# Moving a memset and retuning the constants of a build-time scheduler in a fused attention and MLP kernel

## Chip, cores, metric

One core of a Trainium2 chip. The metric is the device time of one execution in microseconds, as the median over the runs; a profiled execution also gives a span (first to last instruction), about 1.8 us shorter. A ratio between two kernels is the mean time of one kernel's fast runs over that of the other's fast runs of the same rounds, so it is not quite the ratio of the medians quoted beside it.

## The reference

Two branches share one layer-normed input and are added to it: softmax attention with 32 heads of 16, and an MLP that mixes over the sequence.

```python
S, D, H, Dh, F = 2048, 512, 32, 16, 1376
xn  = layernorm(x)
# A: q, k, v = split(xn @ wqkv);  o = softmax(q k^T / sqrt(Dh)) v;  A = o @ wo
# B: h = layernorm(xn);  u = gelu(h^T @ w1 + b1);  B = (u @ w2 + b2)^T
out = x + A + B            # bf16, (1, 2048, 512)
```

The 32 heads' scores are 32 x 2048 x 2048 exponentials. As the profile below shows, they fill one engine, and the matrix products fill another.

## The kernel before

The exponentials are cut into 1024 score tiles of 128x1024. ScalarE takes most of them with its exponential, one per instruction. VectorE takes the others by an integer trick: one instruction from PSUM, and three shifted copies, two usually on GpSimd and one on VectorE. A VectorE tile therefore needs four groups of PV matmuls (the exponentials times V) on TensorE, a ScalarE tile one.

The whole program is laid out at build time by a list scheduler. It walks a model of the five engines with fixed costs, and writes one instruction stream per engine. The engines run their streams in order, so a constant of the model changes what is in the streams. These are the parts that the change touches (cuts marked):

```python
PE_SWITCH = 0.11          # model: TensorE changes between row-tiled scores and column-tiled other work
DMA_I, DMA_L = 0.6, 3.5   # model: issue and landing of a DMA
D_LATE = 1.0              # how late VectorE asks for its next score tile
ACT_MIN = 0.5             # filler matmuls are put in where TensorE's modelled activity is below this
# ...
def est(specs):                        # when could this instruction start
    for s_ in specs:
        r = max(r, sc.ready(s_["eng"], s_["reads"], s_["writes"]))
# ...
def fill(t_next, same):                # matmuls without use, to hold the TensorE clock
    if cur_ext is not None or last_n is None or sc.pe_activity(t_next) > ACT_MIN:
        return
# ...   TensorE's choice: next score tile, or a PV or extra group first?
wants = [sc.free["act"] + EXP_I * i for i in range(4)]
if fly < D_FLY and len(free_p) >= 4 + P_KEEP:
    wants.append(sc.free["dve"] + backlog(sc.free["dve"]) + D_LATE)
need = sorted(wants)[ahead] - 0.46 - DEAD_SLACK
# ...
if pick is not None and pick[0] + pick[4] + PE_SWITCH <= go + PE_FIT:
    pe_c = pick[:4]                    # the group fits before the score tile is due
```

"Extra" work is everything else on TensorE: Q, K and V projections, the MLP's first product ("ut"), and the 16 output tiles ("fin": MLP's second product and the attention output product). Each extra task has a due date, counted in score tiles (0 to 1023).

The head, as code:

```python
ln_sums(1)
warm_up(N_WARM, 5)                                   # 11 matmuls without use
sc.add("pool", lambda e: e.memset(v17_main[:, :, 16:17], 1.0), ...)   # the ones column of V
ln_stats(0)                                          # VectorE statistics, GpSimd 1/sqrt ("rstd")
# ... statistics of tiles 1 to 3, their rstds
for t in range(NPRE):
    ln_norm(t)                                       # VectorE, four normalisations
late_memsets()                                       # GpSimd, zeros in VM
for t in range(NPRE):
    transpose_pe(t, TB[t])
# ... copies to SBUF, Q and K products, first scores, first exponential
```

The softmax here doesn't subtract the row's maximum and nothing guards it: scores larger than these inputs give would overflow.

Of the kernel before, what the change touches and what calls it, by code (L numbers as in the profile page):

```python
# [21 lines left out]
NT = S // 128  # L22
# [3 lines left out]
NQB = 4  # L26
NG = 8
NKT = 16
NBLK = NQB * NG
# [16 lines left out]
NXB = 8  # L46
NW = 2
NPRE = 4
N_WARM = 11


SEM = 0.05
PE_SWITCH = 0.11
PE_LAT = 0.40
EXP_I, EXP_L = 0.903, 1.03
P1_I, P1_L = 1.13, 1.22
TS_I, TS_L = 0.335, 0.42
TT_I, TT_L = 0.60, 0.685
EV_I, EV_L = 0.61, 0.69
DMA_I = 0.6  # L60
DMA_L = 3.5
SH_I, SH_L = 0.62, 0.70
HN_I, HN_L = 0.20, 0.29
OT_I, OT_L = 0.60, 0.685
# [1 line left out]
D_FLY = 3  # L66
D_BACK = 0.5
D_STEAL = 0.3
D_LATE = 1.0
P_KEEP = 4  # L70
DEAD_SLACK = 0.1
PORT_SLACK = 0.5
PE_FIT = 0.05
TABLE = 1.3
LIB_I = 7.2
Q_LEAD = 52
KV_LEAD = 16
HARD_HOLD = 10
LATE_BY = 0
EX_FROM = 34  # L80
EX_RATE = 0.15
EX_EARLY = 10
GELU_GAP = 16
ACT_WIN = 3.42
ACT_MIN = 0.5
# [23 lines left out]
class Sched:  # L109
# [36 lines left out]
            deps = {d for d in deps if d.eng != "pe" or d.is_dma}  # L146
        return deps

    def ready(self, eng, reads, writes, dma=False):

        t = 0.0
        for d in self._deps(eng, reads, writes, dma):
            t = max(t, d.t1 + (SEM if d.eng != eng or d.is_dma else 0.03))
        return t

    def port_time(self, eng, t):
# [150 lines left out]
def bass_parallel_sum__softmax_full_mha__mixer_token_mlp__prompt_kernel(  # L307
# [18 lines left out]
    with ExitStack() as es:  # L326
# [164 lines left out]
        def ln_stats(t):  # L491
            sc.add("dve", lambda e: e.bn_stats(stats[:, t, :], x_sb[:, t, :]),
                   reads=[("x", t)], writes=[("stats", t)], cost=(0.6, 0.69))
            sc.add("dve", lambda e: e.bn_aggr(mv[:, t, 0:2], stats[:, t, :]),
                   reads=[("stats", t)], writes=[("mv", t)], cost=(0.12, 0.18))
            ln_rstd(t, 1)
# [51 lines left out]
        def transpose_pe(t, bk):  # L548
            for ct in range(NCT):
                sc.add("pe", lambda e, ct=ct: e.transpose(  # L550
                    ps_bf[:, bk * 1024 + ct * 128: bk * 1024 + (ct + 1) * 128],
                    xn_sb[:, t, ct * 128:(ct + 1) * 128], ident[:]),
                    reads=[("xn", t), ("ident",)], writes=[("bank", bk)], cost=("F", (0, 1, 2, 3), 0.06))
# [69 lines left out]
               writes=[("rcomp", 0)], cost=(1.4, 1.5))  # L623
        ln_sums(1)
        warm_up(N_WARM, 5)
        sc.add("pool", lambda e: e.memset(v17_main[:, :, 16:17], 1.0), writes=[("Vone",)], cost=(0.5, 0.6))  # L626
        ln_stats(0)
        sc.add("dve", lambda e: e.bn_stats(stats[:, 2, :], x_sb[:, 2, :]), reads=[("x", 2)], writes=[("stats", 2)], cost=(0.6, 0.69))
        sc.add("dve", lambda e: e.bn_aggr(mv[:, 2, 0:2], stats[:, 2, :]), reads=[("stats", 2)], writes=[("mv", 2)], cost=(0.12, 0.18))
        ln_moments(1)  # L630
        ln_rstd(1, 2)
        ln_stats(3)
        for t in range(NPRE):
            ln_norm(t)
        late_memsets()
# [1 line left out]
        TB = (0, 1, 2, 3)  # L637
        for t in range(NPRE):
            transpose_pe(t, TB[t])
        for t in range(NPRE):  # L640
            transpose_copy(t, TB[t], "dve" if t == 2 else "act")
        ln_stats(NPRE)
# [370 lines left out]
        oT_done = set()  # L1013
# [65 lines left out]
        def pv_ready(b):  # L1079

            best = None
            for it in pv_q.get(b, ()):
                if not pv_has(it):
                    continue
                t = sc.last_writer[("pT", it[2])].t1 + SEM
                if best is None or t < best[0]:
                    best = (t, it)
            return best
# [39 lines left out]
        while hard or soft or fins:  # L1128
            tail_ = 0.0
            slack_ = 1e9  # L1130
            for due, cost, *_r in hard:
                tail_ += cost
                slack_ = min(slack_, due - cur - tail_ / EX_RATE)
            nxt = soft[0] if soft else (fins[0] if fins else None)
            if nxt is not None and (not hard or slack_ > nxt[0] / EX_RATE):
                cost, nm, gen, need = (soft or fins).pop(0)
                rel = 0
            else:
                due, cost, nm, gen, need, rel = hard.pop(0)
            cur = max(cur, rel) + cost / EX_RATE  # L1140
            ext_tasks.append((max(rel, cur - cost / EX_RATE - EX_EARLY), cur, nm, gen, need))
            if nm == "ut" and not soft:
                cur += GELU_GAP
        ext_tasks.sort(key=lambda z: z[1])

        def h_mark(t):
# [42 lines left out]
                g["cur"] = (kind, what)  # L1189
                return  # L1190

        def est(specs):
            s0 = specs[0]
            r = 0.0
            for s_ in specs:
                r = max(r, sc.ready(s_["eng"], s_["reads"], s_["writes"]))
            t = max(sc.free[s0["eng"]], r)
            if s0.get("port"):
                t = sc.port_time(s0["eng"], t)
            return t  # L1200
# [21 lines left out]

        def fill(t_next, same):

            if cur_ext is not None or last_n is None or sc.pe_activity(t_next) > ACT_MIN:
                return
            if sc.ready("pe", [], [("bank", EX_BANK)]) > sc.free["pe"]:
                return
            b, kt, qb, G, T, e_ = blk_of(last_n)
            r = 2  # L1230
            if sc.pe_mode == "S" and len(sc.pe_tiles) <= 2 and r not in sc.pe_tiles and not same:
                sc.add("pe", lambda e: e.matmul(
                    bank(EX_BANK), lhsT=KT[32 * r:32 * r + 32, T, 128 * kt:128 * (kt + 1)],
                    rhs=QT[32 * r:32 * r + 32, b % 4, :], start=True, stop=True, tile_position=(32 * r, 0)),
                    reads=[("KTt", T, kt), ("QT", b % 4, r)], writes=[("bank", EX_BANK)], name="fill",
                    cost=("S", (r,), 0.214))
            for _ in range(int((t_next - sc.pe_end - 2 * PE_SWITCH - 0.1) / 0.22)):
                sc.add("pe", lambda e: e.matmul(bank(EX_BANK), lhsT=ident[:], rhs=wo_c[:, 0, :], start=True, stop=True),
                       reads=[("ident",)] + [("wo_c", x, r) for x in range(2) for r in range(4)],
                       writes=[("bank", EX_BANK)], name="fill", cost=("F", (0, 1, 2, 3), 0.22))  # L1240
# [5 lines left out]
        while True:  # L1246
            cands = []

            for g in frees:
                if g["cur"] and g["cur"][0] == "sp":  # L1250
                    w = g["cur"][1][0]
                    cands.append((max(sc.free["sp"], sc.ready("sp", w["reads"], w["writes"], dma=True)), 0, "dma", g))
# [68 lines left out]
                    jobs.append((max(t_c, a[0], sc.ready("pe", [], [("bank", PV_BANK)])), 0 if low else 2, "pv", a[1], 0.107))  # L1321
            if cur_ext and cur_ext["cur"] and cur_ext["cur"][0] == "pe":
                late = next_n - min([cur_ext["due"]] + [z[1] - HARD_HOLD for z in ext_tasks if z[2] in ("qt", "kt", "vt")])
                jobs.append((max(t_c, est(cur_ext["cur"][1])), 1 if late > -LATE_BY else 3, "ext", cur_ext, 0.214))
            pick = None
            if jobs:
                m = min(j[0] for j in jobs)
# [1 line left out]
            if sp_ is not None:  # L1329
                ahead = len(ready_q)  # L1330
# [4 lines that stand above are left out]
                two = sorted(slot_time(z) for z in free_slots)  # L1335
                if sc.pe_mode == "S" and e_s <= sc.pe_end + 0.02:
                    go = e_s
                else:
                    t2 = two[1] if len(two) > 1 else 1e9
                    if len(two) == 1:  # L1340
                        t2 = 1e9
                    go = max(e_s, min(need, t2))
                if pick is not None and pick[0] + pick[4] + (PE_SWITCH if sc.pe_mode == "C" else PE_SWITCH) <= go + PE_FIT:
                    pe_c = pick[:4]
                elif pick is not None or True:
                    pe_c = (max(e_s, go if go < 1e8 else e_s), 0, "score", (next_n, sp_, s_))
            elif pick is not None:
                pe_c = pick[:4]
# [93 lines left out]
            if cur_ext is None:  # L1442
                for i, (rel, due, nm, gen, need) in enumerate(ext_tasks):
                    if rel > next_n:
                        continue
                    if need and need[0] == "ut" and (need[1] != len(u_begun) or len(h_done) < NT):
                        continue
                    if need and need[0] == "fin":
                        if need[1] >= 12 and not (("q", NBLK - 2) in have and (NQB - 1, 1) in oT_done):
                            continue  # L1450
                        if need[1] != fin_next or not all(("g", ft) in have for ft in range(NFT)):
                            continue
                        fin_next += 1
                    if nm == "ut":
                        u_begun.append(need[1])
                    ext_tasks.pop(i)
                    cur_ext = dict(gen=gen, cur=None, due=due, name=nm)
                    step_gen(cur_ext)
                    break
# [62 lines left out]
```

## Time and profile before

| | |
|---|---|
| time | 706.06 us (704.78 to 706.14, 3 runs; 706.02 with the fourth) |
| first exponential on ScalarE | 12.95 us |
| last exponential ends | 691.8 us |
| last PV group issued | 693.0 us |
| end of the span | 704.3 us |
| score tiles on ScalarE / VectorE | 725 / 299 |

From the page of the kernel before: its span, the busy times, the chain of work that ended last, and the groups of the exponentials (busy us and mean ns of one; then idle time before them and what ended most of it).

```profile
span 704.3 us, 29187 instructions
PE 688.5 (98%) x12808; PEld 325.6 (46%) x12808; DVE 607.0 (86%) x879; ACT 680.4 (97%) x744; POOL 391.3 (56%) x666
...
PE 73%; ACT 19%; DVE 3%; issue 2%; SPq 2%; POOL 1%; DVEq 0%; DMA 0%; POOLq 0%
...
L737 ACT ACTIVATE pT<-ps 128x1024 bf16<-128x1024 f32 x522 | 515.4, 1151 | 3.8 <-PE ps L713 3.2
...
L748 DVE TENSOR_SCALAR pT<-ps 128x1024 int16<-128x1024 f32 x207 | 252.9, 1222 | 32.7 <-PE ps L713 23.6
...
L737 ACT ACTIVATE x_sb<-ps 128x1024 bf16<-128x1024 f32 x203 | 221.8, 1159 | 1.1 <-PE ps L713 0.9
...
L748 DVE TENSOR_SCALAR x_sb<-ps 128x1024 int16<-128x1024 f32 x92 | 112.4, 1222 | 15.3 <-PE ps L713 10.8
```

ScalarE has under 5 us of idle before its 725 exponentials: it is full. VectorE has 34.4 us of idle before its 299 tiles that a score matmul ended (23.6+10.8). The chain is mostly TensorE. A busy TensorE is not yet a full one, so look at a short stretch near the end of the body. This is the chain of the kernel before (start us, us, what):

```profile
684.41 0.21 PE ps L810 x4
...
686.57 0.32 PE ps L713 x2
686.89 0.33 PE ps L810 x4
687.22 0.41 PE ps L713 x4
687.64 0.77 PE ps L780 x24
688.41 0.32 PE ps L713 x2
```

From 686.57 on each piece starts where the last one ends, with a period of 1.84 us: two score runs (L713), one extra group (L810), six PV groups (L780). In 1.84 us ScalarE does two tiles and VectorE one. So TensorE and ScalarE are both full here. An extra group that follows a score run costs 0.33 us, while eleven in a row cost 2.55 us, some 0.22 each (below), and the group at 684.41, which follows a PV group in the same tiling mode, costs 0.21: the other 0.10 to 0.12 us go with the change of tiling mode. The Trainium skill ("TensorEngine Tiling (Array Packing)", "Key Properties") says that a change of tiling mode drains TensorE; the trace agrees so far as such a change costs 0.10 to 0.12 us.

The head of the kernel before, from its timeline (start us, us, engine, line, operation). L626 is the V-ones memset, L522 the fourth normalisation, L431 the VM memsets, L601 Q products, L737 the first exponentials:

```profile
2.72 2.29 POOL L626 MEMSET V<- 128x512 bf16 x1
...
7.96 0.87 DVE L522 TENSOR_SCALAR hx<-x_sb,mv 128x512 bf16<-128x512 bf16 x1
...
7.88 0.80 POOL L431 MEMSET VM<- 128x256 bf16 x3
...
10.14 1.48 PE L601 MATMUL ps<-xnT,wq_sb 128*128 128x128 bf16 x12
...
12.95 3.77 ACT L737 ACTIVATE pT<-ps 128x1024 bf16<-128x1024 f32 x4 [0.81 <-PE ps L713]
```

Normalisation 4 takes 0.87 us where the median of the sixteen is 0.38; it lies over three GpSimd memsets and ends 0.15 us after they do. The Q products run 0.107 us apart, and the granted clock in the windows from 9 to 12 us is 0.50: half clock.

The tail of the kernel before, from its timeline. L810 is extra work (the last output tile), L1043 an operation on VectorE that feeds the last matmuls L1059:

```profile
693.12 2.55 PE L810 MATMUL ps<-gT_sb,wblk 128*32 128x512 bf16 x44
...
695.67 0.42 DVE L1043 TENSOR_TENSOR oT<-ps,oC 128x256 bf16<-128x256 f32 x1
695.93 0.39 PE L810 MATMUL ps<-xr,ident 128*32 128x512 bf16 x4
...
698.41 1.03 PE L1059 MATMUL ps<-wo_t,oT 128*128 128x512 bf16 x4
```

VectorE's operands are there at 696.1 us, but TensorE is in the last output tile until 696.3 and, after four other products and six matmuls that only hold the clock (left out), reaches the last products at 698.41.

### The profile page before, as it was taken

The page shows a single profiled execution, that of the slowest core. Times are in us where ns is not written, and L with a number is a line of the kernel's source. Part 1 is how long each engine was busy: PE and PEld are TensorE (multiplying, and loading weights), DVE is VectorE, ACT ScalarE, POOL GpSimd, SP SyncE. Part 2 cuts the span into 40 slices and gives each one's busy share as a digit, 9 for nine tenths or more (in the row PEclk, how much of TensorE's full clock was granted, in tenths as well). Part 3 has the DMA queues.
Part 4 walks back from the last instruction along what each step waited for, and adds up shares of the span by engine and source line. Part 5 has one row for each costly group of instructions (what it writes and reads, how often), then busy time and mean ns, then how long its engine had stood idle before and what let it go on. Part 6 is the DMA issues. An engine that isn't in the chain of part 4 may idle for free.

```text
span 704.3 us, 29187 instructions
## 1 busy us (share of the span) xinstructions
PE 688.5 (98%) x12808; PEld 325.6 (46%) x12808; DVE 607.0 (86%) x879; ACT 680.4 (97%) x744; POOL 391.3 (56%) x666
## 2 busy tenths in 40 slices
PE   7999999999999999999999999999999999999998
PEld 4533544444444454444444454444544444445444
DVE  6968889888897889989889998979899888988886
ACT  5999999999999999999999999999999999999993
POOL 5535446565564636556565674546556564665551
PEclk9999999999999999999999999999999999999999
DMA  7103200221002200211221023112221121222211
GB/s 210 32 19 69 51 23 14 52 49 27 15 14 53 48 23 18 43 36 36 49 42 44 19 47 72 48 39 53 54 55 35 43 66 41 53 55 54 48 43 47
DMA packets 85727, 32.31 MB, mean 46 GB/s; under 512 B 67424, under 2 KB 85600, under 8 KB 85600
## 3 DMA queue, kind: packets, MB, share of 16 engines
q1 hardware_dynamic: 85168, 30.05, 18.4%
q8 instruction: 100, 1.64, 1.0%
q10 hardware_dynamic: 432, 0.39, 0.2%
q14 instruction: 27, 0.22, 0.1%
HBM read 21.76 MB, written 2.35 MB: 34 GB/s over the span
## 4 chain that ended last, share of the span: by engine, by line
PE 73%; ACT 19%; DVE 3%; issue 2%; SPq 2%; POOL 1%; DVEq 0%; DMA 0%; POOLq 0%
PE ps L780 27%; PE ps L713 27%; PE ps L810 15%; ACT pT L737 13%; ACT x_sb L737 4%; SPq L404 2%; PE ps L859 1%; DVE pT L748 1%; ACT gT_sb L914 1%; PE ps L619 0%; DVE oT L1006 0%; PE ps L563 0%; PE ps L550 0%; DVE x_sb L748 0%; POOL V L626 0%
## 5 line engine op out<-in xcount | busy, mean ns | idle before, releaser
L737 ACT ACTIVATE pT<-ps 128x1024 bf16<-128x1024 f32 x522 | 515.4, 1151 | 3.8 <-PE ps L713 3.2
L713 PE MATMUL ps<-QT,KT 32*128 32x512 bf16 x2048 | 291.0, 384 | 5.0 <-ACT pT L737 3.0
L748 DVE TENSOR_SCALAR pT<-ps 128x1024 int16<-128x1024 f32 x207 | 252.9, 1222 | 32.7 <-PE ps L713 23.6
L754 POOL INT64_ADD pT<-pT x307 | 185.6, 613 | 147.1 <-DVE pT L757 80.9
L780 PE MATMUL ps<-pT,V 128*32 128x256 bf16 x4632 | 237.9, 275 | 0.9 <-ACT pT L737 0.6
L737 ACT ACTIVATE x_sb<-ps 128x1024 bf16<-128x1024 f32 x203 | 221.8, 1159 | 1.1 <-PE ps L713 0.9
L713 PEld LDWEIGHTS ps<-QT,KT 32*128 32x128 bf16 x2048 | 86.5, 91 | 179.2 <-ACT pT L737 80.6
L780 PEld LDWEIGHTS ps<-pT,V 128*32 128x32 bf16 x4632 | 109.9, 96 | 68.0 <-issue 52.1
L748 DVE TENSOR_SCALAR x_sb<-ps 128x1024 int16<-128x1024 f32 x92 | 112.4, 1222 | 15.3 <-PE ps L713 10.8
L780 PE MATMUL ps<-x_sb,V 128*32 128x256 bf16 x1856 | 115.1, 275 | 0.3 <-ACT x_sb L737 0.3
L754 POOL INT64_ADD pT<-x_sb x128 | 77.4, 613 | 56.8 <-DVE pT L757 32.6
L754 POOL INT64_ADD x_sb<-pT x114 | 69.4, 613 | 44.8 <-DVE pT L757 31.0
L757 DVE TENSOR_SCALAR pT<-pT 128x1024 int16<-128x1024 int16 x149 | 63.4, 428 | 4.5
L780 PE MATMUL ps<-pT,VM 128*32 128x256 bf16 x884 | 61.2, 274 | 0.0
L810 PE MATMUL ps<-hx,wblk 128*32 128x512 bf16 x688 | 60.5, 384 | 0.0
L810 PE MATMUL ps<-gT_sb,wblk 128*32 128x512 bf16 (+1 forms) x704 | 58.4, 383 | 0.7 <-DVE hx L948 0.7
L780 PEld LDWEIGHTS ps<-x_sb,V 128*32 128x32 bf16 x1856 | 47.3, 96 | 24.2 <-issue 18.1
L754 POOL INT64_ADD x_sb<-x_sb x58 | 35.3, 613 | 28.4 <-DVE pT L757 8.1
L757 DVE TENSOR_SCALAR pT<-x_sb 128x1024 int16<-128x1024 int16 x66 | 27.9, 424 | 2.1
L810 PEld LDWEIGHTS ps<-hx,wblk 128*32 128x32 bf16 x688 | 16.2, 94 | 24.1 <-issue 21.1
L780 PEld LDWEIGHTS ps<-pT,VM 128*32 128x32 bf16 x884 | 23.6, 97 | 6.6 <-issue 6.1
L810 PEld LDWEIGHTS ps<-gT_sb,wblk 128*32 128x32 bf16 (+1 forms) x704 | 16.3, 95 | 20.8 <-issue 16.1
(105 smaller groups left out, 397.4 us busy)
## 6 DMA issues: line engine op xcount, KB each, us to landing
wblk<-in_B_w_dram SPq DMA_DIRECT2D x10, 512.0 KB, 4.6
wblk<-in_B_w_dram SPq DMA_DIRECT2D x16, 320.0 KB, 3.6
oC<-OT SPq DMA_DIRECT2D x248, 16.0 KB, 1.8
denb<-rden_scratch SPq DMA_DIRECT2D x124, 32.0 KB, 2.0
xr<-in_A_x_dram SPq DMA_DIRECT2D x16, 128.0 KB, 2.3
dcomp<-OT SPq DMA_DIRECT2D x124, 2.0 KB, 1.8
QT<-Qall SPq DMA_DIRECT2D x120, 16.0 KB, 1.8
out_dram<-osb SPq DMA_DIRECT2D x14, 128.0 KB, 1.9
```

The lines of the kernel that those rows point to most:

```text
L404: return eng.dma_start(dst, src)
L713: specs.append(dict(eng="pe", fn=lambda e, r=r, bk=bk: e.matmul(bank(bk), lhsT=KT[32 * r:32 * r + 32, T, 128 * kt:128 * (kt + 1)], rhs=QT[ ...
L737: return [dict(eng="act", fn=lambda e: e.activation(buf(pbuf[n]), ps[:, s_ * 1024:(s_ + 1) * 1024], ACTF.Exp, scale=LN2_128), reads=[("ban ...
L748: return dict(eng="dve", fn=lambda e: e.tensor_scalar(buf_i(w), ps[:, s_ * 1024:(s_ + 1) * 1024], IBIAS, 0.0, ALU.add, ALU.max), reads=[(" ...
L754: return dict(eng=eng, fn=lambda e: e.int64_add(buf_i(o).bitcast(I64), buf_i(w).bitcast(I64), SHIFTS[k] * 0x0001000100010001), reads=[("pT ...
L757: return dict(eng=eng, fn=lambda e: e.tensor_scalar(buf_i(o), buf_i(w), float(SHIFTS[k]), 1.0, ALU.add, ALU.mult), reads=[("pT", w)], writ ...
L780: specs.append(dict(eng="pe", fn=lambda e, c=c, h=h, i=i, off=off: e.matmul(bank(PV_BANK)[32 * c:32 * c + 32, 256 * par:256 * par + 256], ...
L810: specs.append(dict(eng="pe", fn=lambda e, c=c, w=w: e.matmul(bank(EX_BANK)[32 * c:32 * c + w, :], lhsT=lhs_of(32 * c, 32 * c + w), rhs=rh ...
L859: specs.append(dict(eng="pe", fn=lambda e, ct=ct, c=c, i=i, t=t: e.matmul(bank(EX_BANK)[32 * c:32 * c + 32, 128 * i:128 * (i + 1)], lhsT=x ...
L914: yield "act", [dict(eng="act", fn=lambda e, ap=ap: e.activation(ap, ap, ACTF.Gelu_apprx_tanh), reads=[("gT", f) for f in fts], writes=[(" ...
```

## The change

The intent: free GpSimd's first rstd from the memset; keep the TensorE clock up in the head; give VectorE its score tiles sooner; have the last output tiles done before the end; let work fed by other engines or by DMA have a margin in the model. The diff, cut to its core:

```diff
-N_WARM = 11
+N_WARM = 13
+N_MID = (1, 1, 1, 2)
-PE_SWITCH = 0.11
+PE_SWITCH = 0.1
-DMA_I = 0.6
-DMA_L = 3.5
+DMA_I = 0.65
+DMA_L = 3.0
+DMA_SLACK = 0.8
+EXT_SLACK = 0.2
+PV_SLACK = 0.1
-D_LATE = 1.0
+D_LATE = 0.5
+Q_GUARD = 8
+FIN_END = 985
+FIN_STEP = 18
@@ head
         warm_up(N_WARM, 5)
-        sc.add("pool", lambda e: e.memset(v17_main[:, :, 16:17], 1.0), writes=[("Vone",)], cost=(0.5, 0.6))
         ln_stats(0)
# ... 
         ln_rstd(1, 2)
         ln_stats(3)
+        sc.add("pool", lambda e: e.memset(v17_main[:, :, 16:17], 1.0), writes=[("Vone",)], cost=(2.28, 2.33))
         for t in range(NPRE):
             ln_norm(t)
# ...
             transpose_pe(t, TB[t])
+            warm_up(N_MID[t], 5)
@@ scheduler
+        for i, z in enumerate(ext_tasks):
+            if z[2] == "fin":
+                due = min(z[1], FIN_END - (NT - 1 - z[4][1]) * FIN_STEP)
+                ext_tasks[i] = (min(z[0], due - 30),) + (due,) + z[2:]
-        def est(specs):
+        def est(specs, slack=0.0):
-                r = max(r, sc.ready(s_["eng"], s_["reads"], s_["writes"]))
+                r = max(r, sc.ready(s_["eng"], s_["reads"], s_["writes"], slack=slack, dma_slack=DMA_SLACK))
-                t = sc.last_writer[("pT", it[2])].t1 + SEM
+                t = sc.last_writer[("pT", it[2])].t1 + SEM + PV_SLACK
# ...   extra tasks
+                    if nm in ("ut", "fin") and any(z[2] == "qt" and z[0] < next_n + Q_GUARD for z in ext_tasks):
+                        continue
-                        if need[1] >= 12 and not (("q", NBLK - 2) in have and (NQB - 1, 1) in oT_done):
+                        if need[1] >= 12 and ("q", NBLK - 2) not in have:
# (smaller hunks left out: query DMAs first on the queue, no fillers once the last output tile has begun)
```

More of the change, by code (lines that the diff above doesn't have):

```diff
@@ L59 @@
 EV_I, EV_L = 0.61, 0.69
-DMA_I = 0.6
-DMA_L = 3.5
+DMA_I = 0.65
[3 more added lines that the diff above has]
+PV_SLACK = 0.1
+GEN_SLACK = 0.0
 SH_I, SH_L = 0.62, 0.70
@@ L68 @@
 D_STEAL = 0.3
-D_LATE = 1.0
+D_LATE = 0.5
 P_KEEP = 4
 DEAD_SLACK = 0.1
+PAIR_WAIT = 0.0
 PORT_SLACK = 0.5
@@ L147, in _deps, with ready @@
         return deps
-    def ready(self, eng, reads, writes, dma=False):
+    def ready(self, eng, reads, writes, dma=False, slack=0.0, dma_slack=0.0):
         t = 0.0
         for d in self._deps(eng, reads, writes, dma):
-            t = max(t, d.t1 + (SEM if d.eng != eng or d.is_dma else 0.03))
+            t = max(t, d.t1 + (SEM + (dma_slack if d.is_dma else slack) if d.eng != eng or d.is_dma else 0.03))
         return t
@@ L1223, in fill @@
         def fill(t_next, same):
-            if cur_ext is not None or last_n is None or sc.pe_activity(t_next) > ACT_MIN:
+            if cur_ext is not None or last_n is None or fin_next == NT or sc.pe_activity(t_next) > ACT_MIN:
                 return
@@ L1247, in bass_parallel_sum__softmax_full_mha__mixer_token_mlp__prompt_kernel @@
             cands = []
-            for g in frees:
+            for g in sorted(frees, key=lambda g: not (g["cur"] and g["cur"][0] == "sp" and g["cur"][1][0]["name"] == "q_row")):
                 if g["cur"] and g["cur"][0] == "sp":
@@ L1323, in bass_parallel_sum__softmax_full_mha__mixer_token_mlp__prompt_kernel @@
                 late = next_n - min([cur_ext["due"]] + [z[1] - HARD_HOLD for z in ext_tasks if z[2] in ("qt", "kt", "vt")])
-                jobs.append((max(t_c, est(cur_ext["cur"][1])), 1 if late > -LATE_BY else 3, "ext", cur_ext, 0.214))
+                jobs.append((max(t_c, est(cur_ext["cur"][1], EXT_SLACK)), 1 if late > -LATE_BY else 3, "ext", cur_ext, 0.214))
             pick = None
@@ L1341, in bass_parallel_sum__softmax_full_mha__mixer_token_mlp__prompt_kernel @@
                         t2 = 1e9
-                    go = max(e_s, min(need, t2))
+                    go = max(e_s, t2 if t2 <= need + PAIR_WAIT else need)
                 if pick is not None and pick[0] + pick[4] + (PE_SWITCH if sc.pe_mode == "C" else PE_SWITCH) <= go + PE_FIT:
```

## The prediction

> **What bounds it now.** Median 706.06 us; profiled span 704.3 us, in three parts.
>
> - Head, to the first exponential on ScalarE at 12.95 us (timeline).
> - Body, to the last exponential at 691.8 us. ScalarE is full: the waits view gives it about 4 us of idle there, and 60 us stretches hold 66 or 67 exponentials, one each 0.917 us. TensorE is full too: the chain of waits is 73% TensorE, and in the end stretch it is contiguous TensorE work with a period of 1.84 us (score runs 0.32+0.41, PV 0.77, one other 0.33), in which ScalarE does two tiles and VectorE one. VectorE is 86% busy and does 299 of 1024 score tiles, 1.22 us each; it waits 34.4 us (82 times) for scores.
> - Tail, from the last PV at 693.3 us to the end, 11 us.
>
> **Head.** The V-ones memset (GpSimd, 2.72 to 5.01 us) delays the first rstd to 5.07 (input ready at 4.13), but the first normalisation sits behind VectorE's own statistics until 6.55, so the move frees only about 0.15 us. The memset (2.29 us) will start as the fourth rstd ends, at about 7.75, just before normalisation 4. The Trainium skill ("SBUF — State Buffer", "SBUF: two separate sides") says that GpSimd and a two-port VectorE operation exclude each other for the whole instruction. This trace agrees: normalisation 4 took 0.87 instead of 0.38 us and ended 0.14 us after three GpSimd memsets did. So normalisation 4 should end near 10.2, not 8.83. Against that, the clock is at half in 8.9 to 12 us (windows), where 32 Q/K matmuls cost 0.107 us each; two more warm-ups and five between the transposes may keep it full, worth about 1.6 us. Net: first exponential at 13.0, 11.5 to 15.
>
> **Body.** Margins (0.8 us on DMA-fed, 0.2 on extra, 0.1 on PV work) change only the build-time order. The stalls they address are small (waits): TensorE's loads wait 6.7 us for GpSimd and 0.5 for a query DMA, VectorE 3.2 for denominators. Asking for VectorE's tile 0.5 us sooner attacks the 34.4 us. If half returned, VectorE could take ten more tiles (about 1.5 us each with its shift), but each costs TensorE three more PV groups (0.32 us), and TensorE is full. I give 5 to 8 more tiles, 2 to 3 us together with the margins.
>
> **Tail.** Output tile 15 is computed after the last PV (693.1 to 696.3, about 3.2 us of TensorE), so final products wait until 698.4, though VectorE's operands are there at 696.1. With it due earlier, the tail should be about 2.2 us shorter, 9 us, but the work moves into a full body and is partly paid there. Net 1.5 to 2 us.
>
> **Predicted: 701.5 us, range 696.5 to 706.5; faster by over 2%: 0.03, within 2%: 0.95, slower: 0.02.**
>
> **What would show it.** Right: normalisation 4 ends within 0.2 us of the memset's end; tail from last PV near 9 us; no output tile after the last PV; VectorE's score waits well below 34 us; 304 to 307 VectorE tiles; ScalarE still full. Wrong: first exponential near 11 us (memset doesn't block, clock stays full); a much higher tile count, which would mean TensorE had room.
>
> **What would make it wrong.** A half clock through the head (first exponential at 15 us); the new order pairing score tiles less well, costing TensorE a mode change each; early output tiles starving PV of buffers; or an order lucky by more than these sums.

## The result

| | before | after |
|---|---|---|
| time, us | 706.02 (4 runs) | 699.63 (699.18 to 701.46, 4 runs) |
| ratio, 95% interval | | 0.9918 (0.9898 to 0.9939) |
| span of the profiled run | 704.3 | 697.7 |
| first exponential | 12.95 | 14.00 |
| last exponential ends | 691.8 | 683.7 |
| last PV group issued | 693.0 | 689.5 |
| from there to the end | 11.3 | 8.2 |
| tiles on ScalarE / VectorE | 725 / 299 | 717 / 307 |

It is 6.4 us faster, 0.8%. The head got slower by 1.05 us. The last exponential ends 8.1 us sooner, but the last PV only 3.5 us sooner, and the tail behind it is 3.1 us shorter. (3.5 and 3.1 make the 6.6 us of the span.) The same views as before, first the page of the kernel after:

```profile
span 697.7 us, 29410 instructions
PE 682.8 (98%) x12914; PEld 312.1 (45%) x12914; DVE 623.2 (89%) x902; ACT 673.4 (97%) x736; POOL 397.2 (57%) x675
...
PE 58%; ACT 36%; DVE 3%; issue 1%; DMA 1%; POOL 0%; SPq 0%; DVEq 0%
...
L747 ACT ACTIVATE pT<-ps 128x1024 bf16<-128x1024 f32 x528 | 516.5, 1130 | 1.9 <-PE ps L723 0.9
L758 DVE TENSOR_SCALAR pT<-ps 128x1024 int16<-128x1024 f32 x220 | 268.7, 1222 | 23.6 <-PE ps L723 18.4
...
L747 ACT ACTIVATE x_sb<-ps 128x1024 bf16<-128x1024 f32 x189 | 203.4, 1136 | 0.5 <-PE ps L723 0.5
...
L758 DVE TENSOR_SCALAR x_sb<-ps 128x1024 int16<-128x1024 f32 x87 | 106.3, 1222 | 12.3 <-PE ps L723 9.5
```

Eight tiles went over to VectorE, whose waits for scores fell from 34.4 to 27.9 us (18.4+9.5) though there are more tiles. ScalarE is still full.

The head, from the timeline of the kernel after (L641 the V-ones memset, L531 normalisation 4, L440 and L442 the VM memsets, L610 Q products):

```profile
7.68 2.27 POOL L641 MEMSET V<- 128x512 bf16 x1
...
7.77 3.10 DVE L531 TENSOR_SCALAR hx<-x_sb,mv 128x512 bf16<-128x512 bf16 x1
...
9.55 1.11 POOL L440 MEMSET VM<- 128x256 bf16 x3
10.61 0.11 POOL L442 MEMSET VM<- 128x16 bf16 x1
...
12.04 0.83 PE L610 MATMUL ps<-xnT,wq_sb 128*128 128x128 bf16 x12
...
14.00 3.77 ACT L747 ACTIVATE pT<-ps 128x1024 bf16<-128x1024 f32 x4 [0.48 <-PE ps L723]
```

Normalisation 4 now lies over the moved memset and over the VM memsets behind it, and takes 3.10 us. In this run the clock was full: twelve Q products took 0.83 us instead of 1.48.

The tail, from the timeline of the kernel after:

```profile
685.82 2.55 PE L820 MATMUL ps<-gT_sb,wblk 128*32 128x512 bf16 x44
...
688.85 0.39 PE L820 MATMUL ps<-xr,ident 128*32 128x512 bf16 x4
...
689.50 0.28 PE L790 MATMUL ps<-pT,VM 128*32 128x256 bf16 x4
...
691.88 1.03 PE L1069 MATMUL ps<-wo_t,oT 128*128 128x512 bf16 x4
```

The last output tile still comes after the last exponential (683.7), but now ahead of the last PV groups. The final products start 2.4 us after the last PV group, not 5.4. There TensorE now waits for VectorE's operands (ready at 691.77); before, they waited for TensorE.

### The profile page after: what moved, and what is told of

Read it like the earlier page. It is cut to its first block, busy times and chain, and to the rows that moved or that the text cites. A ratio compares the mean times of both kernels' runs of the same rounds, so it can differ in the third digit from the quotient of the medians.

```text
span 697.7 us, 29410 instructions
## 1 busy us (share of the span) xinstructions
PE 682.8 (98%) x12914; PEld 312.1 (45%) x12914; DVE 623.2 (89%) x902; ACT 673.4 (97%) x736; POOL 397.2 (57%) x675
## 4 chain that ended last, share of the span: by engine, by line
PE 58%; ACT 36%; DVE 3%; issue 1%; DMA 1%; POOL 0%; SPq 0%; DVEq 0%
ACT pT L747 25%; PE ps L790 23%; PE ps L723 20%; PE ps L820 12%; ACT x_sb L747 10%; DVE pT L758 1%; ACT gT_sb L924 1%; PE ps L869 1%; DMA denb<-rden_scratch 1%; PE ps L628 1%; DVE hx L531 0%; DVE OT L980 0%; DMA x_sb<-in_A_x_dram 0%; DVE wkv_raw L1016 0%; PE ps L559 0%
## 5 line engine op out<-in xcount | busy, mean ns | idle before, releaser
L758 DVE TENSOR_SCALAR pT<-ps 128x1024 int16<-128x1024 f32 x220 | 268.7, 1222 | 23.6 <-PE ps L723 18.4
L723 PE MATMUL ps<-QT,KT 32*128 32x512 bf16 x2048 | 283.5, 384 | 6.2 <-ACT pT L747 3.7
L790 PE MATMUL ps<-pT,V 128*32 128x256 bf16 x4692 | 251.0, 275 | 1.5 <-DVE OT L980 1.2
L764 POOL INT64_ADD pT<-pT x296 | 179.7, 615 | 124.1 <-DVE pT L767 64.9
L747 ACT ACTIVATE x_sb<-ps 128x1024 bf16<-128x1024 f32 x189 | 203.4, 1136 | 0.5 <-PE ps L723 0.5
L723 PEld LDWEIGHTS ps<-QT,KT 32*128 32x128 bf16 x2048 | 76.9, 91 | 184.9 <-ACT pT L747 76.4
L764 POOL INT64_ADD x_sb<-pT x148 | 90.4, 614 | 66.3 <-DVE pT L767 41.0
L758 DVE TENSOR_SCALAR x_sb<-ps 128x1024 int16<-128x1024 f32 x87 | 106.3, 1222 | 12.3 <-PE ps L723 9.5
L767 DVE TENSOR_SCALAR pT<-pT 128x1024 int16<-128x1024 int16 x167 | 71.1, 428 | 4.7
L764 POOL INT64_ADD x_sb<-x_sb x42 | 25.6, 613 | 20.6 <-DVE pT L767 6.8
L790 PEld LDWEIGHTS ps<-pT,VM 128*32 128x32 bf16 x904 | 24.1, 96 | 11.5 <-issue 9.5
```

What stands on the lines that cost most here:

```text
L723: specs.append(dict(eng="pe", fn=lambda e, r=r, bk=bk: e.matmul(bank(bk), lhsT=KT[32 * r:32 * r + 32, T, 128 * kt:128 * (kt + 1)], rhs=QT[ ...
L747: return [dict(eng="act", fn=lambda e: e.activation(buf(pbuf[n]), ps[:, s_ * 1024:(s_ + 1) * 1024], ACTF.Exp, scale=LN2_128), reads=[("ban ...
L758: return dict(eng="dve", fn=lambda e: e.tensor_scalar(buf_i(w), ps[:, s_ * 1024:(s_ + 1) * 1024], IBIAS, 0.0, ALU.add, ALU.max), reads=[(" ...
L764: return dict(eng=eng, fn=lambda e: e.int64_add(buf_i(o).bitcast(I64), buf_i(w).bitcast(I64), SHIFTS[k] * 0x0001000100010001), reads=[("pT ...
L767: return dict(eng=eng, fn=lambda e: e.tensor_scalar(buf_i(o), buf_i(w), float(SHIFTS[k]), 1.0, ALU.add, ALU.mult), reads=[("pT", w)], writ ...
L790: specs.append(dict(eng="pe", fn=lambda e, c=c, h=h, i=i, off=off: e.matmul(bank(PV_BANK)[32 * c:32 * c + 32, 256 * par:256 * par + 256], ...
```

## Experiments

Twelve kernels ran, all correct, five rounds each. "E1" and so on are the names used below. The counts of tiles and of leftover matmuls in the expectations are counts in the built instruction streams.

### E1: the memset behind the normalisations

```diff
         ln_stats(3)
-        sc.add("pool", lambda e: e.memset(v17_main[:, :, 16:17], 1.0), writes=[("Vone",)], cost=(2.28, 2.33))
         for t in range(NPRE):
             ln_norm(t)
+        sc.add("pool", lambda e: e.memset(v17_main[:, :, 16:17], 1.0), reads=[("xn", NPRE - 1)], writes=[("Vone",)], cost=(2.28, 2.33))
         late_memsets()
```

> The kernel after, with the V-ones memset put behind normalisation 4 (it waits for it). Theory A (GpSimd's memset shuts VectorE's normalisation 4 out): normalisation 4 takes about 0.4 us again and ends near 8.2 us instead of 10.87; the first exponential starts at 11.3 us instead of 14.0; the body is in the same order and just comes earlier, so the time is about 2.7 us below the kernel after, near 697.0 us (ratio to before 0.987). Rival B (the late start comes from the extra warm-ups in TensorE's queue or from late data): first exponential still at 13.5 to 14 us, time as the kernel after, ratio 0.992.

Measured: 697.48 us, ratio 0.9874 (0.9856 to 0.9892), span 695.7. From the timeline of E1, normalisation 4 and the first exponentials:

```profile
7.74 0.41 DVE L531 TENSOR_SCALAR hx<-x_sb,mv 128x512 bf16<-128x512 bf16 x1
...
11.29 3.77 ACT L747 ACTIVATE pT<-ps 128x1024 bf16<-128x1024 f32 x4 [0.48 <-PE ps L723]
```

Normalisation 4 is back to 0.41 us and the first exponential starts at 11.29. Theory A holds, and the rival falls: the warm-ups and the loads are the same and do not delay the start. (The edit takes two things out of normalisation 4's way, for the VM memsets come behind the moved one.) Of the 2.7 us at the start 2.0 are left in the span. The rest is lost little by little: the lead over the kernel after is 2.7 us at 42 us, 2.3 at ScalarE's table load at 409 us, and 2.1 at the last exponential; what eats it is open.

### E2: the extra warm-ups undone

```diff
-N_WARM = 13
-N_MID = (1, 1, 1, 2)
+N_WARM = 11
+N_MID = (0, 0, 0, 0)
```

> The kernel after with 11 warm-ups and none between the transposes; the memset stays where the change put it. Theory A: normalisation 4 still ends near 10.9 us, and the granted clock falls to half while TensorE waits, so the Q and K products take 0.107 us each as in the kernel before, and the first exponential starts near 15.5 us: 1.5 us slower than the kernel after (ratio to before 0.994). Rival B (the warm-ups are what delays the start): first exponential near 13 us and faster than the kernel after.

Measured: 701.43 us, ratio 0.9927 (0.991 to 0.9943), span 699.2, first exponential at 14.73 us. The twelve Q products took 1.49 us, half clock. So it is not the warm-ups that delay the start: without them it should have come near 13 us. What they gain is not shown. This profile starts 0.7 us later than the kernel after's, where 1.5 were expected, but the same head with its warm-ups is at half clock too in the profiles of E7 to E9, and starts there at 15.3 to 15.4 us, later than here.

### E3: the whole head of before

```diff
-N_WARM = 13
-N_MID = (1, 1, 1, 2)
+N_WARM = 11
+N_MID = (0, 0, 0, 0)
         warm_up(N_WARM, 5)
+        sc.add("pool", lambda e: e.memset(v17_main[:, :, 16:17], 1.0), writes=[("Vone",)], cost=(0.5, 0.6))
# ... and the moved memset taken out again
```

> The kernel after with the whole head of before (memset ahead of the statistics, 11 warm-ups, none between). Theory A: the change's head costs time by itself, first exponential back at 12.95 us, time 1.0 us below the kernel after (about 698.6 us, ratio 0.9905); all of the gain, 7.5 us of the span, comes from the scheduled body. Rival (the head is part of the gain): ratio 0.993 or higher.

Measured: 699.32 us (697.75 to 699.72), ratio 0.9887 (0.9867 to 0.9907), span 697.6, first exponential at 13.49 us, Q products again at half clock. E2 and E3 differ only in the memset's place: the moved memset costs 2.1 us between their medians. The head is no part of the gain. Against the kernel after as a whole the difference (0.9887 and 0.9918) is not resolved by the intervals; compared by clock, E3's two runs with a mean clock of 1.000 took 697.75 us, and the kernel after's three took 699.2 to 699.7.

### E4: VectorE's score tile asked for as late as before

```diff
-D_LATE = 0.5
+D_LATE = 1.0
```

> The kernel after with VectorE's score tile asked for as late as before (1.0 for 0.5). The built order then has 298 VectorE tiles, not 307, and 726 on ScalarE. Theory C (the gain of the body is tiles moved from ScalarE to VectorE, 0.917 us each, and the last exponential ends that much earlier): last exponential about 8 us later than in the kernel after, near 692 us, no output tile left for after the last scores, time 2 to 6 us above the kernel after, ratio 0.995 to 1.0. Rival D (TensorE alone is the bound, so the number of VectorE tiles doesn't matter): same time as the kernel after, ratio 0.992 within 0.0015.

Measured: 704.36 us, ratio 0.9964 (0.9946 to 0.9981), span 700.6. VectorE has 298 tiles and waits 41.0 us for scores (27.9 in the kernel after). The last exponential ends about 691.7 us, as expected. No output tile is left behind the last PV, and from there to the end it is 8.2 us as in the kernel after. Theory C holds: on top of the rest of the change the sooner tile is worth 3.2 us, give or take 1.9 (difference of the two ratios; 2.9 us of the span). It is not worth the full 8 us by which the exponentials end sooner, because TensorE then has PV groups and output tiles left (from the last exponential's start to the last PV it is 1.9 us here, 7.0 in the kernel after).

### E5: the switch constant alone, on the kernel before

```diff
-PE_SWITCH = 0.11
+PE_SWITCH = 0.1
```

> The kernel before with one constant of its build-time scheduler changed: the assumed cost of a TensorE mode switch, 0.11 to 0.10 us. The built order then has 303 VectorE tiles (before 299) and leaves the same 44 matmuls of an output tile for after the last scores. Theory E (this constant decides whether an extra or PV group still fits ahead of the next score, so TensorE's gaps are filled better, and part of the body's gain is this): last exponential 3 to 4 us earlier than before, ratio to before 0.994 to 0.9955. Rival (a rounding of no effect; the gain is the sooner score tile and the margins): ratio 1.000 within 0.0015.

Measured: 707.17 us (704.02 to 709.51), ratio 1.0019 (0.9999 to 1.004). The expectation missed. VectorE had its 303 tiles, but the last exponential came only 1.3 us sooner. Its runs show mean clocks of 0.983 to 0.990, where the kernel before's beside it show 0.993 to 1.000. The next lines are windows of E5 (us; length; busy us of PE, PEld, DVE, ACT, POOL; then the granted clock, DMA share and GB/s):

```profile
46.00:50.00 4.00, 3.10 (x43) 1.00 (x31) 3.88 (x8) 4.00 (x5) 2.12 (x2) 0.94 0.09 20
50.00:54.00 4.00, 3.97 (x32) 0.97 (x30) 2.98 (x12) 3.99 (x5) 0.61 (x1) 0.50 0.65 144
54.00:58.00 4.00, 4.00 (x52) 1.20 (x48) 3.20 (x4) 3.58 (x4) 1.20 (x2) 0.71 0.86 137
```

TensorE fell to half clock at about 49.5 us and stayed there for some 7 us; it fell again for some 3 us at 261 us, after a stretch (258 to 260 us) in which it was busy for 0.67 of 2 us. The kernel before has four filler matmuls between 48 and 53 us (two of them before 50) and holds a clock of 1.00 in the same windows; the order of E5 has one at 48.8, beside a score run, and two at 52.7, when the clock is already down. That the missing fillers let the clock fall is likely but was not tested: no run put them back. So what the constant is worth by itself was not seen: the lower clock covered it.

### E6: the sooner score tile alone, on the kernel before

```diff
-D_LATE = 1.0
+D_LATE = 0.6
```

> The kernel before with VectorE's score tile asked for sooner, alone (0.6 instead of 1.0; 0.5 alone can't be tried, its two builds differ). The built order has 304 VectorE tiles, but 128 matmuls of output tiles (before 60) are left for after the last scores. Theory E: without the smaller switch constant the sooner scores crowd the extra work out, so output tiles end up behind the last scores; ratio 1.005 to 1.016, slower than before, with a longer stretch from the last exponential to the end. Rival F (five tiles fewer on ScalarE at 0.917 us each are a gain): ratio 0.9935.

Measured: 717.39 us, ratio 1.0172 (1.0159 to 1.0185). It has 304 VectorE tiles, five more than before, and is 12 us slower. Theory E holds and rival F falls. Tiles on VectorE are no gain by themselves. The profiled run has 10.8 us of ScalarE waiting for scores (4.1 before), the last exponential starts at 695.9 us although it has the earliest start of all heads of before (11.6), and two output tiles follow it.

### E7: the switch constant back, on the kernel after

```diff
-PE_SWITCH = 0.1
+PE_SWITCH = 0.11
```

> The kernel after with the switch constant back at 0.11 and everything else of the change kept. The built order has 310 VectorE tiles (after 307), but 376 matmuls of output tiles are left for after the last scores (after 88). Theory E: last exponential near the kernel after's, then some 94 groups of four at 0.22 us, 20 us of TensorE work, less 5 us that the kernel after has there too: 15 to 26 us slower than the kernel after, ratio 1.013 to 1.03. Rival F (more VectorE tiles are faster): ratio 0.989.

Measured: 727.16 us, ratio 1.0308 (1.0295 to 1.0322), 27 us slower than the kernel after. From the timeline of E7, two of the output tiles that TensorE runs after the last PV, and ScalarE's next large instruction (the bracket is idle time before and what ended it):

```profile
696.19 2.56 PE L820 MATMUL ps<-gT_sb,wblk 128*32 128x512 bf16 x44
...
700.41 2.56 PE L820 MATMUL ps<-gT_sb,wblk 128*32 128x512 bf16 x44 [0.80 <-DVE osb L964]
...
723.63 0.60 ACT L1078 ACTIVATE oT<-ps 128x512 bf16<-128x512 f32 x1 [35.26 <-PE ps L1058]
```

ScalarE had been done with exponentials since 688.4 us and sat idle for 35 us. With 0.11 an extra group no longer counts as fitting ahead of the score tile that VectorE now wants sooner; the output tiles are put off, and run one after the other at the end, with waits for VectorE between them (0.80 us in the line shown, up to 1.96 us; before the two longest VectorE had itself waited for a load of `xr`). That this is how the constant acts is read from the code and the leftover counts. A hundredth of a microsecond in a model decides this.

### E8: the output tiles' due dates undone

```diff
-            if z[2] == "fin":
+            if False:
```

> The kernel after without the earlier due dates of the output tiles. The built order has 308 VectorE tiles and leaves 100 output-tile matmuls after the last scores (after: 92). My prediction's theory (the dates shorten the tail, net 1.5 to 2 us): ratio 0.9945 and a tail from the last PV near 11 us again. Rival G (the dates hardly move anything, the tail's gain comes from last PV groups interleaved with the output tile): ratio 0.992 to 0.9935, tail from the last PV within 1 us of the kernel after's 8.1.

Measured: 702.81 us, ratio 0.9956 (0.9944 to 0.9967), span 701.2 with a tail from the last PV of 12.0 us. The prediction's theory holds, rival G falls. From the timeline of E8, the last PV group, then the output tile that the due dates had moved ahead of it:

```profile
689.17 0.28 PE L790 MATMUL ps<-x_sb,VM 128*32 128x256 bf16 x4
689.28 2.55 PE L820 MATMUL ps<-gT_sb,wblk 128*32 128x512 bf16 x44
...
694.58 1.03 PE L1069 MATMUL ps<-wo_t,oT 128*128 128x512 bf16 x4
```

The profiled head was cold and 1.3 us later than the kernel after's (first exponential at 15.3 us), so of 3.5 us of span 2.2 belong to the due dates. The runs with full clock say the same: 701.5 us against 699.5, 2 us. The built orders leave about the same amount of output-tile work after the last score (100 and 92 matmuls); what counts is whether it stands before or after the last PV.

### E9: the margins undone

```diff
-DMA_SLACK = 0.8
-EXT_SLACK = 0.2
-PV_SLACK = 0.1
+DMA_SLACK = 0.0
+EXT_SLACK = 0.0
+PV_SLACK = 0.0
```

> The kernel after with the three margins at zero (DMA-fed, extra and PV work), the rest kept. The built order has 304 VectorE tiles (after 307) and 80 output-tile matmuls left after the last scores (after 92). Theory H (margins keep TensorE and VectorE from running into work that isn't there yet, and let the order that was built be the order that runs): 3 to 6 us slower than the kernel after, ratio 0.996 to 1.0. My prediction's view (the stalls that they address are small, margins worth under 1 us): ratio 0.992 to 0.994.

Measured: 705.75 us (703.96 to 708.34), ratio 0.9993 (0.9972 to 1.0014). All of the gain is gone, and my view of the margins is refuted. But why is only partly shown. Windows of E9, whose profiled run is the slowest of its six, then of the kernel after (columns as in E5):

```profile
50.00:54.00 4.00, 3.07 (x35) 1.09 (x35) 4.00 (x13) 4.00 (x5) 1.15 (x2) 0.81 0.17 42
54.00:58.00 4.00, 3.97 (x36) 0.92 (x32) 2.92 (x9) 3.69 (x5) 0.61 (x1) 0.50 1.26 234
58.00:62.00 4.00, 4.00 (x54) 1.21 (x46) 2.60 (x4) 3.33 (x4) 2.40 (x4) 0.50 0.27 52
62.00:66.00 4.00, 4.00 (x48) 1.21 (x40) 2.58 (x4) 2.53 (x3) 1.20 (x2) 0.50 0.07 13
```

```profile
50.00:54.00 4.00, 3.91 (x42) 1.30 (x39) 4.00 (x16) 4.00 (x6) 0.00 (x0) 1.00 0.31 70
54.00:58.00 4.00, 3.50 (x49) 1.24 (x48) 3.24 (x5) 3.89 (x6) 1.82 (x3) 1.00 1.26 234
58.00:62.00 4.00, 4.00 (x80) 1.72 (x76) 3.38 (x5) 4.00 (x6) 2.40 (x4) 1.00 0.13 28
62.00:66.00 4.00, 4.00 (x72) 1.73 (x72) 3.62 (x6) 4.00 (x5) 2.60 (x5) 1.00 0.06 10
```

E9's TensorE is at half clock from 53 to 66 us; ScalarE, with 2.3 us less busy time in the last three windows, starves for scores, and VectorE loses 3 tiles over the whole kernel. The order of the kernel after has seven filler matmuls between 49 and 54 us, E9's has three: one at 51.2, and two at 55.1, when the clock is already down. (I take it that without margins the model books less waiting for TensorE there and sees no need for fillers; no run tested it.) Half clock is probably not all of it: E9's two fastest runs, with mean clocks of 0.995 and 0.994, took 704.0 and 704.6 us, some 4.5 to 5 us above the kernel after. By my estimate such a mean clock leaves 7 to 8 us at half clock (0.005 or 0.006 of 704 us, over one half), which can cost at most half of that, 3.5 to 4 us. How the loss splits between clock, tiles and stalls is open.

### E10: due dates and sooner tile both undone

```diff
-D_LATE = 0.5
+D_LATE = 1.0
-            if z[2] == "fin":
+            if False:
-                        if need[1] >= 12 and ("q", NBLK - 2) not in have:
+                        if need[1] >= 12 and not (("q", NBLK - 2) in have and (NQB - 1, 1) in oT_done):
```

> The kernel after without the two parts that move tiles: VectorE's score asked for as late as before, and the output tiles' old due dates and gate; the switch constant, the margins, the guard and the head stay. The built order has 298 VectorE tiles and leaves 56 output-tile matmuls (before: 299 and 64). If the two parts are the whole gain: as the kernel before with the change's slower head, ratio 1.000 to 1.003. If switch constant, margins and guard have a gain of their own: ratio 0.996 to 0.999.

Measured: 705.63 us, ratio 0.9995 (0.9979 to 1.0011), span 703.8, tail 10.7 us, first exponential at 13.5. Switch constant, margins, the guard (`Q_GUARD`), the DMA constants, the smaller hunks and the new head together gain nothing that can be told from zero. (The head in it costs 0.5 us at the start of this profile and 2.1 us by E2 and E3, so the others may gain about as much; the guard, the DMA constants and the smaller hunks were never undone alone.) Put the due dates back (E4): 0.9964, 3.2 us of span. Put the sooner tile back as well (the kernel after): 0.9918, another 2.9 us.

### E11 and E12: a version meant to beat both

```diff
 # both: the head of E1, and
-D_LATE = 0.5
+D_LATE = 0.45
 # E11
-PE_SWITCH = 0.1
-FIN_END = 985
-FIN_STEP = 18
+PE_SWITCH = 0.09
+FIN_END = 960
+FIN_STEP = 27
 # E12: PE_SWITCH = 0.095, FIN_END = 960, FIN_STEP = 24
```

> A version meant to beat both: the head of the first experiment, VectorE's score asked for a little sooner still (0.45), the output tiles due earlier (960, 27 apart), switch constant 0.09. The built order has 308 VectorE tiles and no output-tile matmul left for after the last scores. From the counts: against the first experiment one ScalarE tile less (0.9 us) and 92 matmuls of TensorE work, 23 groups of 0.22 us or 5 us, out of the tail, partly paid in the body: 2 to 5 us below it, ratio 0.981 to 0.985. Rival: the smaller constant is below the real gap (0.10 to 0.11 us in the trace), the machine lags the built order, ratio 0.986 or more.

> As the run before, with a switch constant of 0.095 and due dates 960, 24 apart: 308 VectorE tiles, no output-tile matmul left after the last scores, another order. Same theory: ratio 0.982 to 0.986; if the two differ by more than 0.004 the order's details count for as much as these parts.

Measured: E11 693.40 us, ratio 0.9822 (0.9804 to 0.9839); E12 694.27 us, ratio 0.9834 (0.9817 to 0.9852). Both beat the kernel after, whose ratio is 0.9918, and E1, whose ratio is 0.9874. From the timeline of E11, the last PV group and the final products:

```profile
683.45 0.28 PE L790 MATMUL ps<-x_sb,V 128*32 128x256 bf16 x4
...
685.84 1.03 PE L1069 MATMUL ps<-wo_t,oT 128*128 128x512 bf16 x4
```

The first exponential is at 11.5 us, and the last PV is issued about 1 us after the last exponential has started (682.3). No output tile is left there. So TensorE and ScalarE finish together, with 308 VectorE tiles; in the kernel after TensorE ran on for 7 us. The smaller switch constant, though below the measured 0.10 to 0.12, did no harm that shows here; it was not varied alone.

## Why the prediction was right or wrong

**The time** (701.5 us, range 696.5 to 706.5) was right: 699.63. The forecast gain of 4.5 us measured 6.4. The number is in part luck: the terms erred both ways (start of the exponentials 1.05 us later, where 0.05 was forecast; from there to the last PV 4.6 us gained, where the body was to give 2 to 3; tail 3.1 us shorter, not 2.2). And the result hung on constants that I hadn't weighed (below).

**TensorE and ScalarE both full: right.** The exponentials ended 8.1 us sooner and the last PV only 3.5. E4 shows the other side: the sooner tile moved the last exponential by 8 us and the time by 3.

**VectorE's tiles, "5 to 8 more", "2 to 3 us together with the margins": right in count, the term was mis-sized.** It got 8. On top of the rest of the change the sooner tile is worth 3.2 us (E4); on the kernel before, without the rest, it is a loss (E6, with 0.6 for 0.5).

**"The stalls they address are small": this is the step that failed.** I sized the margins by the stalls in the trace of before. Without them the new order gains nothing (E9, 0.9993). A margin in a scheduler does not only save the stall that it is named for: it changes where every later instruction is put, and here also whether fillers are placed. Part of the loss is half clock at 53 to 66 us, shown by the windows; that the fillers make that difference is argued, and the rest of the loss is open.

**The switch constant was not weighed at all.** I took 0.11 to 0.10 for rounding. With 0.11 kept, the same change is 3% slower than before (E7). Alone it shows no gain (E5, whose clock fell), and the sooner tile alone loses 1.7% (E6). The sooner tile pays only together with the other constants.

**The tail, "about 9 us", net 1.5 to 2: right.** It became 8.2 from 11.3 us; undoing the dates costs 2.2 us (E8). The way was a little different: the tile did not move ahead of the last scores, only ahead of the last PV groups.

**The head: mechanism right, size off.** The lock was right: normalisation 4 ended at 10.87 us instead of the 10.2 predicted, because it also waited for the VM memsets that follow at once. (In the profiles of E4, E9 and E10 it got in after the second of the three, and ended 2.8 us after its start, not 3.1.) "Net: first exponential at 13.0" was 14.0 in the profile. E1 proves the cause by taking it away, E2 against E3 prices it at 2.1 us. The Trainium skill ("SBUF — State Buffer", "Who interferes with whom") says that a GpSimd instruction and VectorE's two-port modes exclude each other and that the one issued first wins; in the trace the memset starts at 7.68 and the normalisation at 7.77, and the normalisation lost. That the normalisation runs in a two-port mode is inferred from its being shut out. Not every VectorE instruction is: in the kernel before the same memset (2.72 to 5.01 us) lay over VectorE's statistics, which took 0.69 us under it (at 3.22) and 0.69 without it (at 5.73). So the old place did VectorE no harm.

**The warm-ups: only half right.** I hoped that they "may keep it full". The twelve Q products took 0.83 us in the profiles of the kernel after, E4 and E10, but 1.49 in E7, E8 and E9, which have the same head. The old head shows both as well (E6 0.83; before, E3 and E5 1.48 to 1.49). The Trainium skill ("TensorE: Matmul & The Clock Gate", "Part 1: The HAM clock gate (the "warmup" mystery)") says that the clock follows an activity window that runs free of the kernel's start, and that the number of cold matmuls varies between runs. The runs agree that it varies: the same head of before has its first exponential at 11.6 us in E6 and at 13.5 in E3. That a free-running window is the reason, no run here shows, and three warm profiles of six against one of four are too few to say that the new warm-ups help. With E1's head, which does not leave TensorE idle for 2.5 us, all three profiles (E1, E11, E12) show it between 11.1 and 11.5.

## What to carry to other kernels

When two engines share a port, move the off-path instruction to a place where the other engine has nothing of the locking kind to do, and make it wait there; "later on the same engine" is not enough. In a kernel whose engines are all full, shifting work to an idle one pays only as far as the next full engine can follow, and a shift without the matching deadlines for that engine can cost several times what it was to bring. Judge the constants of a build-time scheduler by the order that comes out (work left behind at the end, fillers, tiles per engine), never by the size of the number changed.

## What the Trainium skill lacked or had wrong

- "SBUF — State Buffer": the lock is told for one instruction. It does not say what a row of GpSimd instructions does. Here VectorE's normalisation, issued at 7.77 us under a memset that took 2.27, did not get in between that and the next memsets either, and ended at 10.87, 0.15 us after the last of them (10.72). In E4, E9 and E10 it did get in, after the second of three short memsets: in E4 it ended at 10.40, and the third memset, begun at 10.21, took 0.45 us instead of 0.31.
- "TensorE: Matmul & The Clock Gate": the clock is said to fall after an idle window of about 3.4 us. In E5 and E9 it fell to half although TensorE counted as busy for 3.10 of 4 us and 3.07 of 4 us in the windows where that happened; how much activity in a window is too little the page does not say. The kernel after, at 3.69 and 3.91 of 4 us in the same two windows, kept it (and so did the kernel before at 3.11 of 4 with four fillers, so the busy column does not tell).
- "TensorEngine Tiling (Array Packing)" gives no figure for the drain at a change of mode: it is 0.10 to 0.12 us here (a group of four takes 0.33 us behind a score run, 0.21 behind a PV group, 0.22 to 0.23 in a row of eleven).
- No page warns that the granted clock in a profile can read 1.00 while matmuls run at half rate; the clock gate's page says only that its trace events were seen to be unreliable. In E2 and E3 the windows from 9 to 14 us read 1.00, and twelve Q products took 1.49 us instead of 0.83.
